# A causal convolution and a two-product mixture step on one core: the denominator's sum moved to an adding transfer, one form of the cubic, two convolution pieces, a new order

## The chip, the cores and the metric

One core of a Trainium2 chip runs the kernel. The time is that of one execution on the device in microseconds (us). The core's engines run side by side, each with its own queue in order: PE (matrix products; its weight loads are shown apart as PEld), ACT (activation functions), DVE (vector operations), POOL (GpSimd, vector operations too) and SP, which here only issues transfers. Transfers run on 16 DMA engines. PE reads from on-chip memory (SBUF) and writes to accumulators (PSUM, eight banks); ACT and DVE reach both, POOL and the transfers SBUF alone.

## The reference

x has 8 sequences of 4096 tokens with 192 columns, in 8 heads of 24. The weights of 7 taps per head are put through a softmax, and each column is convolved with its head's taps, causally. Then every token goes through a two-layer step with a rational function between:

```python
w = softmax(weight)                      # [8 heads, 7 taps]
x = conv(x, w)                           # 32768 tokens x 192
h = x @ w_in                             # 192 -> 2048
P = a[0] + a[1] * h + a[2] * h**2 + a[3] * h**3
Q = 1.0 + np.abs(b[0]) * np.abs(h) + np.abs(b[1]) * h**2
g = P / (Q + 1e-06)
out = g @ w_out                          # 2048 -> 192
```

The product weights come as float64, everything else is float32.

## The kernel before

The 32768 tokens are taken in 64 chunks of 512. For one chunk:

- **Load.** SP loads the chunk's columns (two transfers, `in_xa` and `in_xb`) in a layout with 9 blocks of 58 tokens, each with the 6 tokens ahead of it.
- **Convolution** (L259). It is a matrix product with a band of taps, for six groups of 32 columns. A matmul makes 32 columns of 58 tokens and uses one of PE's four column tiles of 32. Half 0 has four groups on the four column tiles (9 x 4 = 36 matmuls), half 1 has two groups on two column tiles (18). Steps `c0a`, `c0b`, `c0c` are the three pieces of half 0, `c1a` to `c1c` those of half 1. A float32 matmul is two records in the trace. ACT copies the result out (step `xh`, L267), rounded, and DVE subtracts the copy (`xl`, L273 and L277) to get the remainder; of half 1 both lie in one tile, the copy in partitions 0 to 63 and the remainder in 64 to 127.
- **First product** (`g1`, L289). The 2048 columns of h are made in 8 *units* of 2 x 128 columns: a unit's h is 128 partitions x 1024 numbers in two PSUM banks (tile `hp`), from 10 matmuls of 512 tokens. There are two such tiles.
- **Elementwise steps of a unit**, each over 128 x 1024 numbers. The cubic, by Horner's rule in tile `t`: `hs` copies h to SBUF (ACT, L334), `p` makes a3 h + a2 (POOL, L340, or ACT, L328), `u` multiplies by h (POOL, L347, or DVE, L345), `v` adds a1 and multiplies by h (DVE, L351). The denominator: `A` is |b0||h| (ACT, L354), `B` is |b1|h^2 (ACT, L357), `Q` adds B to A (POOL, L360). Its reciprocal: `L` takes the logarithm (ACT, L363), `Y` the exponential of minus that (ACT, L366, tile `y` in PSUM, of which there is one), and with a first product `m` (DVE, L370) the steps `e` (L375) and `g` (L379, both DVE) do one step of refinement and finish the unit's g.
- **Second product** (`g2`, L306). Per unit 128 columns x 2 are multiplied with `w_out`, in pieces `a` to `d`, for two pairs of 128 tokens one after the other; `O` (L313) copies a finished pair out, and SP stores it (L314).

`MODES` says how a unit's cubic begins: U as above on POOL; V has `p` on ACT; H has `p` on ACT and `u` on DVE, without the copy `hs`. `MODES = "UUUHVUUV"` makes five U, one H and two V units in a chunk.

The order in which the program hands steps to the engines is a table, and the scheduler keeps it: each engine runs its steps in that order, and waits for what a step needs (inputs, and a free buffer: 4 each of `t`, `A` and `B`, 3 of `hs`, 11 of `g`, 1 of the convolution's result). `PLAN` is one round of it; a step's number behind the point tells how many chunks it lags behind the chunk that the round begins. 61 rounds are run so. `START` holds the first two rounds, mixed with the preparation of the weights (steps `wi*` and `wo*`: 16 pieces are turned from float64 to float32 by integer operations on ACT, DVE and POOL), and `END` what is left at the end.

Of the kernel before, what the change touches and what calls it, by code (L numbers as in the profile page):

```python
# [62 lines left out]
wim3.0 wid4.0 wih1.0 wid3.0 g10a.0 wio2.0 wim4.0 wir2.0 g10b.0 wis4.0 wia5.0 wio4.0 hs0.0 wil1.0
wis3.0 wir4.0 g11a.0 wio3.0 wih2.0 wir3.0 wih3.0 wim5.0 p0.0 u0.0 wia6.0 g11b.0 B0.0 wil2.0 wis5.0
wil3.0 A0.0 v0.0 wim6.0 hs1.0 Q0.0 wia7.0 wio5.0 wid6.0 wid5.0 p1.0 A1.0 wim7.0 wid7.0 wir5.0 wih4.0
g12a.0 L0.0 woa2.0 wil4.0 wis6.0 wis7.0 g12b.0 wom2.0 wio7.0 c0a.1 Y0.0 c0b.1 B1.0 hs2.0 wio6.0
wih5.0 u1.0 wir6.0 B2.0 c0c.1 A2.0 m0.0 wod2.0 v1.0 p2.0 wir7.0 g13a.0 u2.0 wos2.0 e0.0 g0.0 wil5.0
g13b.0 xh0.1 woa0.0 xl0.1 wih6.0 v2.0 woa1.0 c1a.1 c1b.1 Q1.0 hs3.0 B3.0 wom0.0 g14a.0 wod0.0 A3.0
L1.0 wom1.0 Y1.0 u3.0 Q2.0 woo2.0 wor2.0 g14b.0 v3.0 p4.0 wos1.0 woo1.0 c1c.1 g15a.0 wos0.0 m1.0
woo0.0 wil6.0 e1.0 g15b.0 hs4.0 B4.0 L2.0 Q3.0 g1.0 hs5.0 A4.0 u4.0 v4.0 woa6.0 wih7.0 Y2.0 m2.0  # L70
wom6.0 g16a.0 g16b.0 wod1.0 xh1.1 wod6.0 p5.0 wor0.0 L3.0 B5.0 Q4.0 woa3.0 A5.0 e2.0 g2.0 wor1.0
woa4.0 hs6.0 u5.0 wom3.0 wos3.0 wos6.0 wil7.0 wom4.0 Y3.0 woo6.0 wod3.0 Q5.0 woo3.0 L5.0 L4.0 wos4.0
p6.0 B6.0 v5.0 m3.0 wor6.0 woa7.0 g17a.0 e3.0 g17b.0 xl1.1 g3.0 wod7.0 u6.0 A6.0 v6.0 Y4.0 m4.0
wor3.0 g10a.1 wom7.0 e4.0 g10b.1 hs7.0 wos7.0 p7.0 A7.0 woa5.0 Q6.0 hs0.1 B7.0 g4.0 Y5.0 wom5.0
# [10 lines left out]
L3.2 xl0.1 hs5.2 c1a.1 e1.2 g23c.2 g1.2 v4.2 Y2.2 g23d.2 B5.2 c1b.1 g16a.2 O0.2 p5.2 u5.2 A5.2
g16b.2 m2.2 c1c.1 g24a.2 e2.2 g2.2 g24b.2 hs6.2 Q5.2 B6.2 Y3.2 p6.2 v5.2 m3.2 g24c.2 g24d.2 g25a.2
g17a.2 g25b.2 g17b.2 A6.2 u6.2 g25c.2 e3.2 g25d.2 L5.2 L4.2 g26a.2 Q6.2 xh1.1 g3.2 xl1.1 v6.2 Y4.2
g26b.2 hs7.2 m4.2 p7.2 g10a.1 B7.2 g26c.2 e4.2 A7.2 g10b.1 g4.2 hs0.1 g26d.2 Y5.2 B0.1 u7.2 p0.1
A0.1 g27a.2 g27b.2 L6.2 u0.1 g27c.2 v7.2 g11a.1 g27d.2 O1.2 m5.2 g11b.1 Q7.2 hs1.1 p1.1 e5.2 g20a.1
g5.2 g20b.1 u1.1 Y6.2 v0.1 g20c.1 Q0.1 g12a.1 g20d.1 B1.1 L7.2 g12b.1 m6.2 A1.1 g21a.1 g21b.1 e6.2  # L90
# [6 lines left out]
g17a.1 O1.1 g21a.0 A6.1 L5.1 g17b.1 p6.1 g21b.0 g24a.0 g24b.0 Y5.1 u6.1 g24c.0 g21c.0 Q6.1 g21d.0
p7.1 m5.1 g24d.0 g25a.0 g22a.0 g25b.0 A7.1 g22b.0 g25c.0 B7.1 e5.1 g25d.0 g26a.0 L6.1 g26b.0 g5.1
Y6.1 v6.1 m6.1 hs7.1 g22c.0 g26c.0 Q7.1 g26d.0 g22d.0 L7.1 e6.1 g6.1 g23a.0 u7.1 g27a.0 g23b.0 Y7.1
v7.1 m7.1 e7.1 g7.1 g27b.0 g27c.0 g27d.0 g23c.0 O1.0 g23d.0 O0.0  # L100
# [8 lines left out]
def kernel(  # L109
# [143 lines left out]
    GROUPS = ((0, 1, 2, 3), (4, 5))  # L253

    def conv_part(c, half, cps, blks):
        for blk in blks:
            for j, g in enumerate(GROUPS[half]):
                n = min(BW, CH - blk * BW)
                nc.tensor.matmul(cps[32 * j:32 * j + 32, blk * BW:blk * BW + n], lhsT=stat(c, blk, g),  # L259
                                 rhs=wb_t[:, g, 0:n], start=True, stop=True, tile_position=(0, 32 * j))  # L260

    X = {}

    def conv_evac_act(c, half, cps):
# [2 lines left out]
        nc.scalar.copy(out=xh[0:n], in_=cps[0:n])  # L267
        X[c, "AB"[half]] = xh

    def conv_evac_dve(c, half, cps):  # L270
        if half == 0:
            xl = xpool.tile([P, CH], F32R, name="xl")
            nc.vector.tensor_tensor(out=xl, in0=cps, in1=X[c, "A"].bitcast(F32), op=ALU.subtract)  # L273
            X[c, "L"] = xl
        else:
# [1 line left out]
            nc.vector.tensor_tensor(out=xh[64:P], in0=cps[0:64], in1=xh[0:64].bitcast(F32), op=ALU.subtract)  # L277

# [80 lines left out]
    def step_Q(k):  # L359
        nc.gpsimd.tensor_tensor(out=st[k]["A"], in0=st[k]["A"], in1=st[k]["B"], op=ALU.add)  # L360
# [128 lines left out]
```

## Time and profile before

| | |
|---|---|
| median of 3 runs | 2807.57 us (2807.32 to 2807.76) |
| span of the profiled execution, which is also its time | 2807.8 us |
| PE, DVE, ACT, POOL busy | 2748.3, 2683.3, 2688.4, 2684.4 us |
| one round of 512 tokens | 42.68 us |
| DMA: bytes moved, share of the 16 engines | 64.43 MB, 8.4% |

A row of the list of groups gives line, engine, operation, output and inputs by tile name, shapes and count, then busy time in us and the mean of one in ns, then how long the engine stood idle just before them and who ended that. Busy times of neighbouring instructions overlap a little, since an engine starts the next one while the last one is still writing; for PE more so. What an instruction costs its engine is therefore read from start to start, and the rows of the timeline give starts. In the timeline a row with "x24" stands for 24 records in a row.

### The profile page before, as it was taken

The page shows a single profiled execution, that of the slowest core. Times are in us where ns is not written, and L with a number is a line of the kernel's source. Part 1 is how long each engine was busy: PE and PEld are TensorE (multiplying, and loading weights), DVE is VectorE, ACT ScalarE, POOL GpSimd, SP SyncE. Part 2 cuts the span into 40 slices and gives each one's busy share as a digit, 9 for nine tenths or more (in the row PEclk, how much of TensorE's full clock was granted, in tenths as well). Part 3 has the DMA queues.
Part 4 walks back from the last instruction along what each step waited for, and adds up shares of the span by engine and source line. Part 5 has one row for each costly group of instructions (what it writes and reads, how often), then busy time and mean ns, then how long its engine had stood idle before and what let it go on. Part 6 is the DMA issues. An engine that isn't in the chain of part 4 may idle for free.

```text
span 2807.8 us, 50193 instructions
## 1 busy us (share of the span) xinstructions
PE 2748.3 (98%) x20224; PEld 2458.2 (88%) x20224; DVE 2683.3 (96%) x2309; ACT 2688.4 (96%) x2990; POOL 2684.4 (96%) x1304
## 2 busy tenths in 40 slices
...
PEclk8899999999999999999999999999999999999999
...
DMA packets 49193, 64.43 MB, mean 23 GB/s; under 512 B 4672, under 2 KB 43840, under 8 KB 48960
## 3 DMA queue, kind: packets, MB, share of 16 engines
q1 hardware_dynamic: 48960, 61.22, 7.9%
q8 instruction: 159, 2.61, 0.4%
...
## 4 chain that ended last, share of the span: by engine, by line
PE 96%; DVE 2%; issue 1%; ACT 0%; DMA 0%; SPq 0%; ACTq 0%; DVEq 0%
PE op L306 48%; PE hp L289 42%; PE cps L259 6%; DVE ad L227 0%; PE cps L306 0%; DVE t L351 0%; DVE wl_t L245 0%; DMA g<-in_w_in 0%; DVE g L370 0%; DVE y L375 0%; DVE tr L233 0%; DVE tr L237 0%; DVE wo_t L233 0%; DVE g L379 0%; DVE wo_t L237 0%
## 5 line engine op out<-in xcount | busy, mean ns | idle before, releaser
L306 PE MATMUL op<-wo_t,g 128*128 128x192 f32 x8128 | 1420.8, 326 | 0.0
L306 PEld LDWEIGHTS op<-wo_t,g 128*128 128x128 f32 x8128 | 1344.6, 189 | 43.9
L360 POOL TENSOR_TENSOR A<-A,B 128x1024 f32<-128x1024 f32 x512 | 1219.2, 2388 | 28.4 <-ACT B L357 26.1
L347 POOL TENSOR_TENSOR t<-t,hs 128x1024 f32<-128x1024 f32 x448 | 1077.9, 2406 | 48.6 <-ACT hs L334 16.3
L289 PE MATMUL hp<-xh,wh_t 128*128 128x512 f32 x2048 | 872.9, 426 | 45.9 <-DVE t L351 41.4
L370 DVE SCALAR_TENSOR_TENSOR g<-t,cf,y 128x1024 f32<-128x1024 f32 x512 | 654.4, 1278 | 57.0 <-ACT y L366 46.6
L351 DVE SCALAR_TENSOR_TENSOR t<-t,cf,hp 128x1024 f32<-128x1024 f32 x512 | 652.5, 1274 | 32.7 <-POOL t L347 29.9
L379 DVE SCALAR_TENSOR_TENSOR g<-y,g 128x1024 f32<-128x1024 f32 x512 | 626.9, 1224 | 17.5
L289 PE MATMUL hp<-xh,wl_t 128*128 128x512 f32 x2048 | 637.7, 393 | 0.0
L375 DVE SCALAR_TENSOR_TENSOR y<-A,y 128x1024 f32<-128x1024 f32 x512 | 625.5, 1222 | 0.0
L363 ACT ACTIVATE B<-A 128x1024 f32<-128x1024 f32 x512 | 547.0, 1069 | 0.2 <-POOL A L360 0.2
L366 ACT ACTIVATE y<-B 128x1024 f32<-128x1024 f32 x512 | 528.8, 1033 | 15.6 <-DVE g L379 14.6
L354 ACT ACTIVATE A<-hp 128x1024 f32<-128x1024 f32 x512 | 528.0, 1031 | 15.8 <-PE hp L289 15.7
L357 ACT ACTIVATE B<-hp 128x1024 f32<-128x1024 f32 x512 | 528.7, 1033 | 0.0
L289 PEld LDWEIGHTS hp<-xh,wh_t 128*128 128x128 f32 x2048 | 388.8, 190 | 124.4 <-DVE t L351 32.6
L334 ACT COPY hs<-hp 128x1024 f32<-128x1024 f32 x448 | 457.2, 1020 | 35.4 <-PE hp L289 34.1
L289 PEld LDWEIGHTS hp<-xh,wl_t 128*128 128x128 f32 x2048 | 388.2, 190 | 87.5
L289 PE MATMUL hp<-xl,wh_t 128*128 128x512 f32 x1024 | 405.5, 396 | 2.4 <-DVE xl L273 2.4
L340 POOL TENSOR_SCALAR t<-hs,cf 128x1024 f32<-128x1024 f32 x320 | 389.6, 1217 | 10.8 <-ACT hs L334 3.9
L328 ACT ACTIVATE t<-hp,cf 128x1024 f32<-128x1024 f32 x192 | 214.7, 1118 | 25.3 <-PE hp L289 22.8
L259 PEld LDWEIGHTS cps<-wb_t,xs 128*32 128x32 f32 x6876 | 162.5, 149 | 65.8 <-issue 64.3
L289 PEld LDWEIGHTS hp<-xl,wh_t 128*128 128x128 f32 x1024 | 195.4, 191 | 23.7 <-DVE xl L273 2.9
...
## 6 DMA issues: line engine op xcount, KB each, us to landing
out<-ob SPq DMA_DIRECT2D x128, 192.0 KB, 2.0
...
g<-in_w_in SPq DMA_DIRECT2D x8, 512.0 KB, 9.4
...
```

The costliest lines, as they stand in the source:

```text
L289: nc.tensor.matmul(H[k][:, j, :], lhsT=w[:, i, part, j, :], rhs=x, start=(n == 0), stop=(n == len(terms) - 1))
L306: nc.tensor.matmul(op[:, t, 0:D], lhsT=g[:, f % 2, tok:tok + P], rhs=wo_t[:, f, :], start=(f == 0 and t == 0), stop=(f == FT - 1 and t == 1))
L347: nc.gpsimd.tensor_tensor(out=t, in0=t, in1=st[k]["hs"], op=ALU.mult)
L351: nc.vector.scalar_tensor_tensor(out=t, in0=t, scalar=a1, in1=flat(k), op0=ALU.add, op1=ALU.mult)
L354: nc.scalar.activation(out=tile_of(k, "A", work), in_=flat(k), func=AF.Abs, scale=r_be0)
L357: nc.scalar.activation(out=tile_of(k, "B", work), in_=flat(k), func=AF.Square, scale=r_sq1)
L360: nc.gpsimd.tensor_tensor(out=st[k]["A"], in0=st[k]["A"], in1=st[k]["B"], op=ALU.add)
L363: nc.scalar.activation(out=st[k]["B"], in_=st[k]["A"], func=AF.Ln, bias=C_Q)
L366: nc.scalar.activation(out=tile_of(k, "y", ps_y), in_=st[k]["B"], func=AF.Exp, scale=-1.0)
L370: nc.vector.scalar_tensor_tensor(out=G[k].rearrange("p a b -> p (a b)"), in0=st[k]["t"], scalar=a0, in1=st[k]["y"], op0=ALU.add, op1=ALU.mult)
L375: nc.vector.scalar_tensor_tensor(out=y, in0=st[k]["A"], scalar=C_Q, in1=y, op0=ALU.add, op1=ALU.mult)
L379: nc.vector.scalar_tensor_tensor(out=g, in0=st[k]["y"], scalar=2.0, in1=g, op0=ALU.subtract, op1=ALU.mult)
```

## The change

Four things are changed together.

1. `Q`: the addition of B to A on POOL is replaced by a transfer that POOL issues, from SBUF to SBUF, with addition at its destination. The data are 128 x 1024 float32, 512 KB, per unit.
2. `MODES` is all U: `hs` on ACT, `p` and `u` on POOL in all eight units.
3. Each half of the convolution is one piece. Half 1 uses four column tiles: its two groups for blocks 0 to 4 on the first two (partitions 0 to 63 of the result, tokens 0 to 289), for blocks 5 to 8 on the other two (partitions 64 to 127, tokens 290 to 511). Its copy and its subtraction are two instructions each, of 64 partitions x 290 and x 222; the remainder goes into the other 64 partitions of the same tokens.
4. `PLAN`, `START` and `END` are written anew.

```diff
-MODES = "UUUHVUUV"
+MODES = "UUUUUUUU"
...
-c0a.0 L7.2 m6.2 u1.1 g12a.1 O1.2 A1.1 e6.2 g12b.1 B1.1 Q0.1 g6.2 g20a.1 hs2.1 c0b.0 v1.1 g20b.1 Y7.2
+c0.0 O1.2 Q1.1 hs2.1 v1.1 Y7.2 p2.1 g20a.1 B2.1 m7.2 g20b.1 u2.1 g13a.1 A2.1 e7.2 L0.1 g13b.1 g7.2 xh0.0
...
-    def conv_part(c, half, cps, blks):
-        for blk in blks:
-            for j, g in enumerate(GROUPS[half]):
-                n = min(BW, CH - blk * BW)
-                nc.tensor.matmul(cps[32 * j:32 * j + 32, blk * BW:blk * BW + n], lhsT=stat(c, blk, g),
-                                 rhs=wb_t[:, g, 0:n], start=True, stop=True, tile_position=(0, 32 * j))
+    CUT = -(-NBLK // 2)
+    TOK = CUT * BW
+
+    def conv_part(c, half, cps):
+        if half == 0:
+            tiles = [(blk, g, g) for blk in range(NBLK) for g in range(4)]
+        else:
+            tiles = [(b + s * CUT, g, 2 * s + g - 4) for b in range(CUT) for s in range(2) for g in (4, 5)
+                     if b + s * CUT < NBLK]
+        for blk, g, j in tiles:
+            n = min(BW, CH - blk * BW)
+            nc.tensor.matmul(cps[32 * j:32 * j + 32, blk * BW:blk * BW + n], lhsT=stat(c, blk, g),
+                             rhs=wb_t[:, g, 0:n], start=True, stop=True, tile_position=(0, 32 * j))
...
+    LOW, UP = (slice(0, 64), slice(0, TOK)), (slice(64, P), slice(TOK, CH))
...
-        n = 32 * len(GROUPS[half])
-        nc.scalar.copy(out=xh[0:n], in_=cps[0:n])
+        if half == 0:
+            nc.scalar.copy(out=xh, in_=cps)
+        else:
+            for p in (LOW, UP):
+                nc.scalar.copy(out=xh[p], in_=cps[p])
...
-            nc.vector.tensor_tensor(out=xh[64:P], in0=cps[0:64], in1=xh[0:64].bitcast(F32), op=ALU.subtract)
+            for p, q in ((LOW, (slice(64, P), LOW[1])), (UP, (slice(0, 64), UP[1]))):
+                nc.vector.tensor_tensor(out=xh[q], in0=cps[p], in1=xh[p].bitcast(F32), op=ALU.subtract)
...
     def step_Q(k):
-        nc.gpsimd.tensor_tensor(out=st[k]["A"], in0=st[k]["A"], in1=st[k]["B"], op=ALU.add)
+        nc.gpsimd.dma_start(out=st[k]["A"], in_=st[k]["B"], accum_op=ALU.add)
...
-    def conv_step(c, half, piece):
-        if piece == 0:
-            if half == 0 and 0 < c < NCH - 1:
-                load_x(c + 1)
...
+    def conv_step(c, half):
+        if half == 0 and 0 < c < NCH - 1:
+            load_x(c + 1)
```

How the order moves shows at three places. On PE, the later two pieces of half 0 before (`cps` is the convolution's result, `op` the second product's, `hp` h; a row here is a matmul, half the records of the trace):

```order
L289 MATMUL hp<-xh_11965,wl_t 128x512
L306 MATMUL op<-wo_t,g 128x192 x2
L259 MATMUL cps<-wb_t,xs_98 32x58 x12
L306 MATMUL op<-wo_t,g 128x192 x2
L259 MATMUL cps<-wb_t,xs_98 32x58 x8
L259 MATMUL cps<-wb_t,xs_98 32x48 x4
L289 MATMUL hp<-xh_11848,wh_t 128x512
```

And PE at half 0 after the change:

```order
L298 MATMUL hp<-xh_12088,wl_t 128x512
L263 MATMUL cps<-wb_t,xs_98 32x58 x32
L263 MATMUL cps<-wb_t,xs_98 32x48 x4
L315 MATMUL op<-wo_t,g 128x192 x4
L298 MATMUL hp<-xh_11919,wh_t 128x512
```

The 36 matmuls of half 0 now stand in one row, between a first and a second product.

On POOL, two units before, the second of them one whose linear step is not on POOL:

```order
L340 TENSOR_SCALAR t<-hs,cf 128x1024
L347 TENSOR_TENSOR t<-t,hs 128x1024
L360 TENSOR_TENSOR A<-A,B 128x1024
L347 TENSOR_TENSOR t<-t,hs 128x1024
L360 TENSOR_TENSOR A<-A,B 128x1024
```

And POOL after it, where `DMA` is the issue of the adding transfer:

```order
L356 TENSOR_TENSOR t<-t,hs 128x1024
L349 TENSOR_SCALAR t<-hs,cf 128x1024
L369 DMA A<-B 128x1024
L356 TENSOR_TENSOR t<-t,hs 128x1024
L369 DMA A<-B 128x1024
L349 TENSOR_SCALAR t<-hs,cf 128x1024
```

Each unit now has a linear step, a product and an issue on POOL, in a changing order.

On ACT, from the step B of a chunk's last unit to that unit's logarithm, before (B, A, then L5, hs, Y5, A, B, L6, hs, Y6, and the unit's own L):

```order
L357 ACTIVATE B<-hp 128x1024
L354 ACTIVATE A<-hp 128x1024
L363 ACTIVATE B<-A 128x1024
L334 COPY hs<-hp 128x1024
L366 ACTIVATE y<-B 128x1024
L354 ACTIVATE A<-hp 128x1024
L357 ACTIVATE B<-hp 128x1024
L363 ACTIVATE B<-A 128x1024
L334 COPY hs<-hp 128x1024
L366 ACTIVATE y<-B 128x1024
L363 ACTIVATE B<-A 128x1024
```

And the same stretch after, where B is the later of the two inputs:

```order
L366 ACTIVATE B<-hp 128x1024
L343 COPY hs<-hp 128x1024
L375 ACTIVATE y<-B 128x1024
L366 ACTIVATE B<-hp 128x1024
L363 ACTIVATE A<-hp 128x1024
L372 ACTIVATE B<-A 128x1024
L343 COPY hs<-hp 128x1024
L375 ACTIVATE y<-B 128x1024
L372 ACTIVATE B<-A 128x1024
```

The logarithm of the unit before has moved ahead of the unit's A and B, so seven instructions stand between its inputs and its logarithm, where eight stood.

More of the change, by code (lines that the diff above doesn't have):

```diff
@@ new lines @@
+g20c.1 hs3.1 v2.1 g20d.1 Y0.1 g21a.1 p3.1 g21b.1 A3.1 m0.1 g14a.1 Q2.1 B3.1 e0.1 u3.1 g14b.1 L1.1 g0.1
+g21c.1 hs4.1 g21d.1 Q3.1 Y1.1 v3.1 g22a.1 g22b.1 B4.1 p4.1 m1.1 g22c.1 A4.1 g15a.1 u4.1 e1.1 L2.1 g15b.1
+g1.1 g22d.1 hs5.1 Q4.1 v4.1 g23a.1 Y2.1 g23b.1 p5.1 xl0.0 g23c.1 B5.1 m2.1 g23d.1 u5.1 L3.1 g16a.1 e2.1
+O0.1 A5.1 g16b.1 g2.1 Q5.1 g24a.1 hs6.1 v5.1 g24b.1 Y3.1 g24c.1 p6.1 c1.0 A6.1 m3.1 u6.1 g17a.1 L4.1
+e3.1 xh1.0 g17b.1 B6.1 g3.1 g24d.1 hs7.1 g25a.1 xl1.0 g25b.1 Y4.1 p7.1 v6.1 g25c.1 A7.1 g25d.1 m4.1 Q6.1
@@ L63 @@
[L63 to L74, printed above, removed]
@@ new lines @@
+B1.0 p1.0 g12b.0 wil3.0 wih4.0 c0.1 u1.0 A2.0 wim6.0 wil4.0 hs2.0 wis6.0 A1.0 p2.0 wio6.0 wid7.0 wim7.0
+L0.0 wir5.0 v1.0 Y0.0 Q1.0 wis7.0 g13a.0 woa0.0 u2.0 B2.0 m0.0 g13b.0 wom0.0 e0.0 hs3.0 Q2.0 wid6.0
+wio7.0 p3.0 B3.0 g0.0 L1.0 wir7.0 wos0.0 Y1.0 wir6.0 woo0.0 A3.0 v2.0 u3.0 wih5.0 m1.0 woa1.0 g14a.0
+woa2.0 xh0.1 wil5.0 g14b.0 wod0.0 Q3.0 wom1.0 hs4.0 wor0.0 e1.0 A4.0 p4.0 v3.0 wih7.0 woa3.0 xl0.1
+g15a.0 wod1.0 g1.0 B4.0 g15b.0 wom2.0 Q4.0 L3.0 wom3.0 wos1.0 u4.0 wih6.0 hs5.0 wos2.0 wil7.0 A5.0 p5.0
@@ new lines @@
+L2.0 wos3.0 woo1.0 B5.0 u5.0 wil6.0 Y2.0 v4.0 wor1.0 m2.0 g16a.0 woa4.0 woo3.0 g16b.0 e2.0 hs6.0 g2.0
+p6.0 woo2.0 Y3.0 v5.0 u6.0 B6.0 wom4.0 g17a.0 wod3.0 wos4.0 A6.0 m3.0 Q5.0 g17b.0 wod2.0 wod4.0 Q6.0
+c1.1 e3.0 L4.0 wor3.0 hs7.0 g3.0 wor2.0 xh1.1 woo4.0 A7.0 v6.0 wor4.0 woa5.0 Y4.0 p7.0 xl1.1 B7.0 wom5.0
+g10a.1 u7.0 m4.0 woa6.0 L5.0 g10b.1 e4.0 L6.0 Q7.0 g4.0 wod5.0 v7.0 Y5.0 wod6.0 wom6.0 g11a.1 woa7.0
+wos5.0 hs0.1 m5.0 g11b.1 A0.1 p0.1 e5.0 B0.1 u0.1 L7.0 wom7.0 woo5.0 hs1.1 wos6.0 B1.1 wos7.0 p1.1 g5.0
@@ L85 @@
[L85 to L90, printed above, removed]
@@ L97 @@
[L97 to L100, printed above, removed]
+c0.1 O1.3 Q1.2 hs2.2 v1.2 Y7.3 p2.2 g20a.2 B2.2 m7.3 g20b.2 u2.2 g13a.2 A2.2 e7.3 L0.2 g13b.2 g7.3
+g20c.2 hs3.2 v2.2 g20d.2 Y0.2 g21a.2 p3.2 g21b.2 B3.2 m0.2 g21c.2 u3.2 A3.2 g21d.2 e0.2 g14a.2 L1.2 g0.2
@@ new lines @@
+Y5.2 p0.1 g27c.2 m5.2 g27d.2 u0.1 g11a.1 O1.2 e5.2 B0.1 g11b.1 L6.2 g5.2 Q0.1 g20a.1 hs1.1 v0.1 g20b.1
+Y6.2 g20c.1 p1.1 g20d.1 L7.2 m6.2 g12a.1 u1.1 A1.1 e6.2 g12b.1 B1.1 g6.2 g21a.1 hs2.1 g21b.1 v1.1 Y7.2
+g21c.1 p2.1 g21d.1 B2.1 m7.2 g22a.1 Q1.1 A2.1 g13a.1 e7.2 u2.1 L0.1 g13b.1 g7.2 g22b.1 hs3.1 Q2.1 v2.1
+g22c.1 Y0.1 g22d.1 p3.1 g23a.1 A3.1 m0.1 g14a.1 u3.1 B3.1 e0.1 g14b.1 L1.1 g0.1 g23b.1 hs4.1 Q3.1 g23c.1
+v3.1 Y1.1 g23d.1 p4.1 g20a.0 O0.1 m1.1 L2.1 g20b.0 u4.1 g24a.1 e1.1 A4.1 g24b.1 B4.1 g15a.1 g1.1 Q4.1
```

50 lines of the change are left out of this document (23 added, 27 removed).

## The prediction

> **What bounds the kernel now.** I read the page first: the span, the busy shares and the chain that ended last.
>
> ```profile
> span 2807.8 us, 50193 instructions
> ...
> PE 2748.3 (98%) x20224; PEld 2458.2 (88%) x20224; DVE 2683.3 (96%) x2309; ACT 2688.4 (96%) x2990; POOL 2684.4 (96%) x1304
> ...
> PEclk8899999999999999999999999999999999999999
> ...
> PE 96%; DVE 2%; issue 1%; ACT 0%; DMA 0%; SPq 0%; ACTq 0%; DVEq 0%
> ```
>
> Four engines are at 96% or more, but the chain is PE for 96% of the span, so PE sets the end. The clock row is at full speed behind the first two slices. Next come the waits between 200 and 2600 us, and the busy time of one round of 512 tokens, from one copy of an output to the same copy a round later.
>
> ```profile
> PEld cps L259 <- issue: 50.4, 224, 0.2
> DVE g L370 <- ACT y L366: 35.8, 113, 0.5
> DVE t L351 <- POOL t L347: 26.4, 110, 0.4
> POOL A L360 <- ACT B L357: 24.1, 57, 0.5
> ```
>
> ```profile
> 1404.03:1446.71 42.68, 42.68 (x318) 38.26 (x317) 41.07 (x36) 41.61 (x48) 41.52 (x21) 1.00 0.08 21
> ```
>
> A round takes 42.68 us. The columns behind it are PE, PEld, DVE, ACT and POOL: PE is busy in all of it, the other three leave only 1.1 to 1.6 us. PE itself waits for no engine; its one gap, in front of the convolution (L259), is its own, 224 times, four a round. So the round is the sum of PE's starts, and the others fit with little to spare. In the start it is otherwise:
>
> ```profile
> 0.00:124.00 124.00, 68.15 (x495) 53.71 (x496) 113.83 (x119) 89.36 (x118) 95.09 (x58) 0.81 0.25 77
> ```
>
> There DVE, with the weights to prepare, is busy for 113.83 of 124 us and PE for 68: what PE saves there is not seen.
>
> **The convolution, the term that pays.** These are PE's rows around a piece of the second half (x36) and three of the first (x24), and a long stretch of the second product.
>
> ```profile
> 1405.94 2.11 PE L306 MATMUL op<-wo_t,g 128*128 128x192 f32 x12
> 1407.98 1.29 PE L259 MATMUL cps<-wb_t,xs 128*32 128x58 f32 x36
> 1409.20 0.50 PE L289 MATMUL hp<-xh,wh_t 128*128 128x512 f32 x1
> ...
> 1424.74 0.59 PE L259 MATMUL cps<-wb_t,xs 128*32 128x58 f32 x24
> 1425.26 0.50 PE L289 MATMUL hp<-xh,wh_t 128*128 128x512 f32 x1
> ...
> 1427.67 0.81 PE L306 MATMUL op<-wo_t,g 128*128 128x192 f32 x4
> 1428.41 0.59 PE L259 MATMUL cps<-wb_t,xs 128*32 128x58 f32 x24
> 1428.93 0.92 PE L306 MATMUL op<-wo_t,g 128*128 128x192 f32 x4
> 1429.78 0.58 PE L259 MATMUL cps<-wb_t,xs 128*32 128x58 f32 x24
> ...
> 1437.55 4.06 PE L306 MATMUL op<-wo_t,g 128*128 128x192 f32 x24
> 1441.32 0.53 PE L289 MATMUL hp<-xh,wh_t 128*128 128x512 f32 x1
> ```
>
> From start to next start, the x36 piece takes 1.22 us and an x24 piece 0.52. A matmul here is two records. The x36 runs on two column tiles, so it is 18 steps; the x24 runs on four, so it is 6. The difference gives (1.22 - 0.52) / 12 = 0.058 us a step, whether two or four tiles work in it, and 0.52 - 6 x 0.058 = 0.17 us fixed. Around a piece more is lost: four records of the second product take 4 x (1441.32 - 1437.55) / 24 = 0.63 us in a long stretch, but 0.74 ahead of a piece and 0.85 between two, so about 0.11 on either side. A piece costs 0.17 + 0.22 = 0.39 us beside its steps. The change makes two pieces of four, which is 0.78 us, and ten steps of the second half's 18 (nine blocks become five positions, two records each), which is 0.46. Together 1.24 us; I take 1.2, because a piece between two kinds of product may lose a little less than one inside the second product. PE's round becomes 41.5 us.
>
> **What the other engines then hold.** The page's groups that are added or removed, and two more from the list of groups by shape:
>
> ```profile
> L360 POOL TENSOR_TENSOR A<-A,B 128x1024 f32<-128x1024 f32 x512 | 1219.2, 2388 | 28.4 <-ACT B L357 26.1
> L347 POOL TENSOR_TENSOR t<-t,hs 128x1024 f32<-128x1024 f32 x448 | 1077.9, 2406 | 48.6 <-ACT hs L334 16.3
> ...
> L340 POOL TENSOR_SCALAR t<-hs,cf 128x1024 f32<-128x1024 f32 x320 | 389.6, 1217 | 10.8 <-ACT hs L334 3.9
> L328 ACT ACTIVATE t<-hp,cf 128x1024 f32<-128x1024 f32 x192 | 214.7, 1118 | 25.3 <-PE hp L289 22.8
> ```
>
> ```profile
> L345 DVE TENSOR_TENSOR t<-t,hp 128x1024 f32<-128x1024 f32 x64 | 77.4, 1210 | 0.0
> L277 DVE TENSOR_TENSOR xh<-cps,xh 64x512 fp32r<-64x512 f32 x63 | 43.1, 683 | 2.0
> ```
>
> ACT loses two linear steps a round (the V units, 2 x 1.12) and its copy of the second half becomes two smaller ones; I give that 0.3 us, between nothing and a whole copy again. The H unit's linear step becomes a copy of about the same length. 41.61 - 2.24 + 0.3 = 39.7. DVE loses the H unit's product (1.21) and gains a second subtraction, between nothing and 0.68, say 0.25, since both together cover the same 512 columns: 41.07 - 1.21 + 0.25 = 40.1. Both stay under 41.5, with about the slack that they have now.
>
> POOL loses eight adds (8 x 2.39 = 19.1) and gains one product (2.41) and three linear steps (3 x 1.22): 41.52 - 19.1 + 2.4 + 3.7 = 28.5 us, plus the issue of eight transfers. No row shows POOL issuing one. The nearest rows are SP's:
>
> ```profile
> 1404.54 0.38 SPq L314 DMA_DIRECT2D out<-ob  x1
> 1409.31 0.47 SPq L158 DMA_DIRECT2D xs<-in_xa  x1
> 1409.84 0.59 SPq L159 DMA_DIRECT2D xs<-in_xb  x1
> ```
>
> The low end is 0.38 us. The high end is the add's own 2.39, which would give POOL 47.6 us a round and the kernel 61 x (47.6 - 42.68) = 300 us more. I take 1.2, twice SP's dearest row, because a transfer that adds names two rows to read and one to write: POOL 38.1 us. The value hardly matters until (41.5 - 28.5) / 8 = 1.62 us, and the time is the old one at (42.68 - 28.5) / 8 = 1.77.
>
> **The transfer.** It replaces a step that ended 2.39 us after its start. Its issue waits on POOL for both of ACT's results, as the add did, with the next unit's linear step and product queued behind it; for its landing wait ACT's logarithm (L363, and behind it all of ACT) and later DVE's correction (L375). SP's loads and stores keep their places beside the convolution and the output copy. How fast transfers are, two stretches of the start show (the last two columns: share of the 16 engines, GB/s), then the page's issues (us to landing):
>
> ```profile
> 10.00:20.00 10.00, 3.11 (x40) 2.12 (x32) 8.77 (x14) 8.05 (x14) 2.71 (x3) 1.00 1.03 348
> 20.00:30.00 10.00, 4.77 (x17) 3.44 (x15) 9.83 (x10) 5.74 (x8) 7.55 (x5) 0.94 1.08 322
> ```
>
> ```profile
> out<-ob SPq DMA_DIRECT2D x128, 192.0 KB, 2.0
> ...
> g<-in_w_in SPq DMA_DIRECT2D x8, 512.0 KB, 9.4
> ```
>
> With the DMA engines full (share over 1) they moved 322 to 348 GB/s. 192 KB landed in 2.0 us, of which 0.6 is moving, so 1.4 is fixed. 0.52 MB is then 1.6 us of all engines if a row read and added counts once, and 3.1 if both rows read count. The low end of the landing is 3.0 us, the high end the 9.4 of the queued weights; I take the doubled reading, because the add needs both rows in the transfer: 1.4 + 3.1 = 4.5, and 5.7 with the issue. Against it stands what ACT does meanwhile:
>
> ```profile
> 1404.39 1.05 ACT L357 ACTIVATE B<-hp 128x1024 f32<-128x1024 f32 x1
> ...
> 1409.05 1.06 ACT L354 ACTIVATE A<-hp 128x1024 f32<-128x1024 f32 x1
> ```
>
> Five starts between these two make (1409.05 - 1404.39) / 5 = 0.93 us an instruction. ACT's new order has seven to eleven of them between the later of A and B and its unit's logarithm: 6.5 us at the tightest, mostly over 8. With one product ahead of the issue on POOL (2.4) the transfer needs up to 8.1. So in a full round ACT hardly waits, and has 1.8 us of slack for it. A landing of 9.4 would be 4 us beyond the tightest place; the distance spans some three units, so there would be two or three such waits a round, about 10 us: 51.5 a round, 3345 us. Per round the engines are taken for 8 x 3.1 plus today's 0.08 x 42.68 = 3.4: 28 of 41.5 us.
>
> The Trainium skill (DMA: Bandwidth & Descriptors, section on the anatomy of a GpSimd DMA) gives 2.0 us plus the bytes at 436 GB/s, which is an estimate of 3.2 us for 512 KB; and Collectives: The Full Stack (section on the bandwidth ceiling) says that a reduce is half as fast as a copy because it reads two sources, not because of the add. Together 4.4 us, the same sum as by my 4.5, where the row of 9.4 gives 3345; no run here shows an adding transfer yet.
>
> **The sum.** 61 full rounds x 1.2 = 73 us off. The first and last units' chains grow by 5.7 - 2.4 = 3.3 us each, partly covered: 5 us on. From the span, 2807.8 (0.2 over the runs' median of 2807.57): 2807.6 - 73 + 5 = 2739.6 us.
>
> **Rivals.** *The issue on POOL is dear (the other side).* At 2.0 us POOL needs 44.5 a round and everything waits on it: 2807.6 + 61 x 1.8 = 2918. For it speaks that POOL can be held by DVE in the start:
>
> ```profile
> 12.86 1.29 POOL L241 TENSOR_TENSOR tr<-tr,ad 128x512 int32<-128x512 int32 x1 [8.73 <-ACT xh L267]
> ...
> 12.60 0.42 DVE L227 TENSOR_SCALAR ad<-ad 128x512 f32<-128x512 f32 x1
> 13.05 1.38 DVE L233 TENSOR_SCALAR tr<-ad 128x512 uint32<-128x512 uint32 x1
> ```
>
> The DVE step that met POOL's add took 1.38 instead of 0.42 and ended 0.28 us behind the add. If DVE's big steps (1.2 us, nearly without a break) held the issue so, each would wait half of one more, 1.2 + 0.6 = 1.8. Against it: in full rounds POOL's steps keep their 2.4 and 1.2 us while DVE is 96% busy. It decides from 1.77. The Trainium skill (SBUF — State Buffer, "Who interferes with whom") says that two-port forms such as tensor_scalar lock GpSimd out for a whole instruction; the start agrees, and the full rounds' DVE instructions are of other forms.
>
> *The DMA engines become the bound.* If an added row costs three passes (1.57 MB) at the page's mean, 61.22 MB in 7.9% of the span, 276 GB/s, a transfer takes 5.7 us; 8 x 5.7 + 3.4 = 49 a round, 3190 us. It decides from (42.68 - 3.4) / 8 = 4.9 us. Against it: 322 GB/s above.
>
> ```profile
> q1 hardware_dynamic: 48960, 61.22, 7.9%
> ```
>
> *The gain is eaten in part.* DVE's 40.1 of 41.5, or late landings, cost half a microsecond to one a round: 2765 to 2800. Here too belongs that the change doesn't do what it says: if the second half's four tiles went two abreast, only 0.78 a round is left, 2765.
>
> **Chances.** The forecast, 2725 to 2765: 0.68 (the low end has 64 rounds and a start relieved by 5 us). Eaten in part: 0.10. No change: 0.04. Dear issue: 0.09. DMA-bound: 0.09. A difference under 0.2% (5.6 us) can't be told from none. Faster 0.78, same 0.04, slower 0.18. The range 2725 to 2830 takes in the first three and the mild third of the fourth, about 0.83.
>
> **What would show it.** Right: a round of 41.3 to 41.7 us with PE busy throughout, L259's gap 128 times instead of 256, POOL down to about two thirds busy without its issues, DMA share near 0.65. Wrong in a size: POOL's issues over 1.62 us back to back; ACT's logarithm waiting for the landing; a DMA share near 1.

## The result, and the profile after

The changed kernel takes 2743.18 us (median of 4 runs, 2740.07 to 2745.52), the kernel before 2807.66 on the same chip. The ratio is 0.9769, with a 95% interval of 0.9755 to 0.9783: 64.5 us or 2.3% faster, 3 us from the 2740 foretold.

The page of the changed kernel: the span, the busy shares, the clock and DMA rows in 40 slices, the two DMA queues and the chain that ended last.

```profile
span 2740.2 us, 51286 instructions
...
PE 2683.1 (98%) x20224; PEld 2420.2 (88%) x20224; DVE 2618.3 (96%) x2309; ACT 2563.2 (94%) x2926; POOL 2305.8 (84%) x1560
...
PEclk7899999999999999999999999999999999999999
DMA  6466566666656666666665666666566666666654
...
q0 software_dynamic: 73728, 268.47, 52.0%
q1 hardware_dynamic: 48960, 61.22, 8.0%
...
PE 95%; DVE 2%; issue 1%; POOL 1%; ACT 1%; DMA 0%; SPq 0%; POOLq 0%; DVEq 0%; ACTq 0%
```

PE still is the chain, with 95% of a shorter span, and its busy time fell by 65.2 us. POOL is no longer at 96%. A new queue, q0, carries the 512 adding transfers and takes half of the DMA engines' time; the DMA row shows five to six tenths in the full rounds, and the clock row stands at full speed from the third slice on, as before.

One round of the changed kernel, from an output copy to the same copy a round later (PE, PEld, DVE, ACT, POOL, granted clock, DMA share, GB/s):

```profile
1413.00:1454.58 41.58, 41.58 (x318) 37.63 (x317) 40.02 (x36) 39.63 (x46) 35.58 (x25) 1.00 0.61 122
```

The round went from 42.68 to 41.58 us. Over the whole run its median is 41.59 against 42.67, so 61 rounds give 61 x 1.08 = 66 of the 67.6 us by which the profiled span is shorter. Nearly nothing lies outside of them: the first output copy comes 0.9 us earlier (122.8 instead of 123.7), the stretch behind the last one is as long as it was (3.7 and 3.6 us).

PE's rows around the two pieces of the convolution in the changed kernel, which answer to the x36 and x24 rows of before:

```profile
1416.63 0.84 PE L263 MATMUL cps<-wb_t,xs 128*32 128x58 f32 x36
1417.40 0.50 PE L298 MATMUL hp<-xh,wh_t 128*128 128x512 f32 x1
...
1435.20 1.34 PE L263 MATMUL cps<-wb_t,xs 128*32 128x58 f32 x72
1436.46 1.57 PE L315 MATMUL op<-wo_t,g 128*128 128x192 f32 x8
```

Half 1 on four tiles takes 0.77 us instead of 1.22, half 0 in one piece 1.26 instead of 3 x 0.52 = 1.56. That is 0.75 us from the pieces themselves. The rest of the round's 1.08 lies beside them. Adding up PE's rows from start to next start over 20 rounds, from 800 us on, gives the second product 20.05 us a round instead of 20.59, since it is cut less often (0.54 less), but the first product 19.51 instead of 19.30 (0.21 more): -0.75 - 0.54 + 0.21 = -1.08. Why the first product is slower in the new order isn't shown.

The waits of the changed kernel between 200 and 2600 us (total, times, longest):

```profile
POOL t L349 <- ACT hs L343: 256.6, 339, 1.7
ACT hs L343 <- PE hp L298: 98.2, 173, 0.8
DVE g L379 <- ACT y L375: 55.4, 119, 1.0
POOL A L369 <- ACT A L363: 45.4, 99, 0.6
PEld cps L263 <- issue: 32.7, 113, 0.4
```

Before the convolution PE's own gap comes 113 times instead of 224, but each is now 32.7 / 113 = 0.29 us instead of 0.23. POOL's room shows as a wait for ACT's copy `hs`, 256.6 / 57.7 rounds = 4.4 us a round. No engine waits long for the transfer: the page's groups of the changed kernel, with its issue and the logarithm that needs it, and the issues' time to landing:

```profile
L372 ACT ACTIVATE B<-A 128x1024 f32<-128x1024 f32 x512 | 550.9, 1076 | 4.2 <-DMA A<-B 4.2
...
L369 POOL DMA_DIRECT2D A<-B x512 | 479.8, 938 | 69.4 <-ACT A L363 53.2
...
A<-B POOLq DMA_DIRECT2D x512, 512.0 KB, 4.8
```

512 logarithms waited 4.2 us in all. An issue takes 0.94 us in the mean (median 0.88, 0.85 to 1.18) and the sum has landed 4.8 us after the issue began.

### The profile page after: what moved, and what is told of

It reads as the page before. It is cut to its first block, busy times and chain, and to the rows that moved or that the text cites. A ratio compares the mean times of both kernels' runs of the same rounds, so it can differ in the third digit from the quotient of the medians.

```text
span 2740.2 us, 51286 instructions
## 1 busy us (share of the span) xinstructions
PE 2683.1 (98%) x20224; PEld 2420.2 (88%) x20224; DVE 2618.3 (96%) x2309; ACT 2563.2 (94%) x2926; POOL 2305.8 (84%) x1560
## 4 chain that ended last, share of the span: by engine, by line
PE 95%; DVE 2%; issue 1%; POOL 1%; ACT 1%; DMA 0%; SPq 0%; POOLq 0%; DVEq 0%; ACTq 0%
PE op L315 48%; PE hp L298 42%; PE cps L263 5%; DVE t L360 0%; PE cps L315 0%; POOL t L356 0%; DVE ad L224 0%; DVE y L384 0%; DVE wl_t L242 0%; DVE g L379 0%; DVE tr L230 0%; POOL t L349 0%; DMA xs<-in_xb 0%; DVE tr L234 0%; ACT ad L220 0%
## 5 line engine op out<-in xcount | busy, mean ns | idle before, releaser
L315 PEld LDWEIGHTS op<-wo_t,g 128*128 128x128 f32 x8128 | 1342.0, 190 | 39.7
L356 POOL TENSOR_TENSOR t<-t,hs 128x1024 f32<-128x1024 f32 x512 | 1267.3, 2475 | 31.8
L349 POOL TENSOR_SCALAR t<-hs,cf 128x1024 f32<-128x1024 f32 x512 | 648.4, 1266 | 302.5 <-ACT hs L343 296.6
L343 ACT COPY hs<-hp 128x1024 f32<-128x1024 f32 x512 | 524.4, 1024 | 133.5 <-PE hp L298 122.1
L375 ACT ACTIVATE y<-B 128x1024 f32<-128x1024 f32 x512 | 536.1, 1047 | 9.7 <-DVE g L388 5.4
L369 POOL DMA_DIRECT2D A<-B x512 | 479.8, 938 | 69.4 <-ACT A L363 53.2
L263 PEld LDWEIGHTS cps<-wb_t,xs 128*32 128x32 f32 x6876 | 122.8, 151 | 37.1 <-issue 36.6
L263 PE MATMUL cps<-wb_t,xs 128*32 128x58 f32 x6876 | 139.2, 229 | 0.0
```

The source lines that it names most:

```text
L315: nc.tensor.matmul(op[:, t, 0:D], lhsT=g[:, f % 2, tok:tok + P], rhs=wo_t[:, f, :], start=(f == 0 and t == 0), stop=(f == FT - 1 and t == 1))
L349: nc.gpsimd.tensor_scalar(tile_of(k, "t", work), st[k]["hs"], a3, a2, ALU.mult, ALU.add)
L356: nc.gpsimd.tensor_tensor(out=t, in0=t, in1=st[k]["hs"], op=ALU.mult)
L375: nc.scalar.activation(out=tile_of(k, "y", ps_y), in_=st[k]["B"], func=AF.Exp, scale=-1.0)
```

## The experiments

The question was which of the four parts carry the 64 us: the shorter convolution alone, with the other parts as bystanders (theory 1), or the parts only together. Each kernel was measured against the kernel before; its ratio stands with its 95% interval.

### The convolution alone

The kernel before, with the new convolution and nothing else; the order keeps its rows, a merged piece standing where its first stood.

```diff
-c0a.0 L7.2 m6.2 u1.1 g12a.1 O1.2 A1.1 e6.2 g12b.1 B1.1 Q0.1 g6.2 g20a.1 hs2.1 c0b.0 v1.1 g20b.1 Y7.2
-c0c.0 p2.1 L0.1 m7.2 g13a.1 B2.1
+c0.0 L7.2 m6.2 u1.1 g12a.1 O1.2 A1.1 e6.2 g12b.1 B1.1 Q0.1 g6.2 g20a.1 hs2.1 v1.1 g20b.1 Y7.2
+p2.1 L0.1 m7.2 g13a.1 B2.1
...
-... v5.1 c1a.0 c1b.0 L4.1 c1c.0 p6.1
+... v5.1 c1.0 L4.1 p6.1
```

> The kernel before with the convolution of the change alone (two pieces, four column tiles); its order, its adds on POOL and its three forms of the cubic stay, with each half's piece where the first of its three stood. Theory 1 (PE's sum of starts sets the round, and each part of the change pays by itself): 1.1 us a round less, 2807.6 - 61 x 1.1 = 2741 us. Rival (before, POOL's starts add up to 8 x 2.36 + 7 x 2.36 + 5 x 1.28 = 41.8 us a round, so POOL takes over as soon as PE is shorter): at the best 41.8 to 42.0 a round, 2755 to 2765. Second rival (the old order was fitted to the old pieces, and the longer piece meets its neighbours at the wrong moment): no gain, 2800 or more.

2842.02 us, ratio 1.012 (1.0105 to 1.0136): 34 us *slower* than before. Its page and its waits between 200 and 2600 us:

```profile
PE 2723.4 (96%) x20224; PEld 2413.9 (85%) x20224; DVE 2689.8 (95%) x2373; ACT 2692.4 (95%) x3054; POOL 2681.9 (94%) x1304
...
POOL 34%; PE 21%; DVE 20%; issue 16%; ACT 8%; DMA 0%; POOLq 0%; SPq 0%; DVEq 0%; ACTq 0%
```

```profile
DVE g L380 <- ACT y L376: 75.5, 56, 1.4
ACT hs L344 <- PE hp L299: 61.4, 55, 1.2
PEld hp L299 <- DVE t L361: 57.4, 55, 1.1
...
POOL A L370 <- ACT B L367: 38.6, 56, 0.7
```

PE's busy time did fall, by 25 us, and still the run is longer. The chain goes round POOL, PE, DVE and ACT: once a round (55 and 56 times) PE waits for DVE's `v` to free a tile of h, ACT for that tile, POOL for ACT's `B`, DVE for ACT's `y`. No engine is full: the round is 43.24 us in the median, while ACT, the fullest beside PE, is busy for 41.7 of it, and POOL's starts add up to 41.8. Half 1's second copy and second subtraction lengthen ACT's and DVE's busy time by only 0.1 us a round, so their size doesn't explain the loss either. What is left is the order: the steps as they stood, with PE's work moved, seem to form a circle that is longer than any engine's sum. That is read from the chain and the waits; no run moved a single step of the old order. Theory 1 falls here.

### Half 1 on two tiles again

```diff
-            tiles = [(b + s * CUT, g, 2 * s + g - 4) for b in range(CUT) for s in range(2) for g in (4, 5)
-                     if b + s * CUT < NBLK]
+            tiles = [(b, g, g - 4) for b in range(NBLK) for g in (4, 5)]
```

(The copies and subtractions keep their sizes and read partitions 0 to 63.)

> The changed kernel with the second half of the convolution on two column tiles again, still one piece: 18 steps for 10. Theory 1 (0.058 us a step, PE sets the round): 8 x 0.058 x 61 = 28 us more than the changed kernel, 2771. Rival (other engines have become the bound at 41.6 us, or PE's steps on two tiles are covered): under 10 us more.

2771.65 us, ratio 0.9871 (0.9856 to 0.9887); the round is 42.07 us, 0.48 more. The eight steps (18 against 10) cost 0.06 us each, as the rows of before gave (0.058).

### Half 0 in three pieces again

```diff
-c0.0 O1.2 Q1.1 hs2.1 v1.1 Y7.2 p2.1 g20a.1 B2.1 m7.2 g20b.1 u2.1
+c0a.0 O1.2 Q1.1 hs2.1 v1.1 Y7.2 p2.1 g20a.1 c0b.0 B2.1 m7.2 g20b.1 c0c.0 u2.1
```

> The changed kernel with half 0 of the convolution in three pieces again, the second and third behind the next two pieces of the second product. Theory 1 (a piece costs 0.25 to 0.39 us of PE beside its steps): two more pieces, 61 x 0.5 to 0.78 = 30 to 48 us more, 2773 to 2791. Rival (what was gained came from POOL and the order, and a piece costs only the 0.2 us of its gap): 61 x 0.4 = 24 us or less.

2787.45 us, ratio 0.9924 (0.9909 to 0.9939); the round is 42.31 us, 0.72 more, 0.36 for each piece. The gap ahead of the convolution in this kernel is back to 225 times:

```profile
PEld cps L263 <- issue: 57.8, 225, 0.4
```

With the experiment before, the two parts of the convolution are worth 28 + 44 = 72 us in the new order, against 64.5 for the whole change: on PE the gain is all the convolution, and the first product's 0.21 us a round goes the other way.

### Half 0 between two pieces of the second product

To see whether a piece costs more between two kinds of product, `c0` was moved behind `g20b`, and the output copy `O1` ahead so that it doesn't have to wait.

```diff
-c0.0 O1.2 Q1.1 hs2.1 v1.1 Y7.2 p2.1 g20a.1 B2.1 m7.2 g20b.1 u2.1
+Q1.1 hs2.1 v1.1 Y7.2 p2.1 g20a.1 B2.1 m7.2 g20b.1 c0.0 u2.1
...
-... L7.1 m6.1
+... L7.1 O1.1 m6.1
```

> The changed kernel with the first half's piece moved behind the next two pieces of the second product, so that it stands in front of a first product as the second half's does, and with the copy of the finished output (O1) moved up behind that chunk's last logarithm. In the changed kernel's rows the piece in front of a second product costs 0.42 us beside its steps (1.265 - 18 x 0.058 = 0.22, 0.09 ahead, 0.11 behind), that in front of a first product 0.25. If the neighbour sets that cost: 61 x 0.17 = 10 us less, 2733. If a piece costs the same anywhere: 2743 as the changed kernel, or a little more where the second product now waits for the copy of its bank.

2744.63 us, ratio 0.9771 (0.9758 to 0.9785): no change. The gap ahead of the convolution in this kernel became smaller,

```profile
PEld cps L263 <- issue: 25.6, 114, 0.2
```

and nothing was won. By PE's rows over 20 rounds the first product takes 0.08 us a round less here than in the changed kernel and the second 0.12 more, so the cost moved from one neighbour to the other. The likely reason, which is only argued: the switch between the two products, at which the piece stood, is now a place of its own. A gap named in the list of waits isn't by itself a cost that can be saved.

### The three forms kept

The changed kernel with the old forms of the cubic (five U, one H, two V); the order stays the new one.

```diff
-MODES = "UUUUUUUU"
+MODES = "UUUHVUUV"
```

> The changed kernel with the three forms of the cubic as before (one H and two V units a chunk), in the new order; a linear step stands on ACT where POOL's stood, and the H unit's on ACT in place of its copy. Theory A (sums: an engine binds when its own work exceeds PE's 41.6 us a round): ACT 39.6 + 2.1 = 41.7, DVE 40.0 + 1.2 = 41.2, POOL falls to 29: 41.8 to 42 a round, 2755 to 2770 us. Theory B (the order decides: what the convolution alone showed, a step put where the order left no room for it makes PE wait): 43 or more a round, 2830 or more.

2833.16 us, ratio 1.0091 (1.0074 to 1.0108). A round of this kernel, its chain and the first of its waits:

```profile
1394.69:1437.65 42.96, 42.38 (x321) 37.53 (x324) 41.06 (x37) 41.42 (x48) 29.80 (x21) 1.00 0.60 119
```

```profile
ACT 37%; issue 32%; DVE 18%; POOL 10%; PE 3%; POOLq 0%; DMA 0%; SPq 0%; ACTq 0%; DVEq 0%
```

```profile
POOL t L358 <- ACT t L337: 368.8, 112, 5.5
POOL A L371 <- ACT B L368: 206.3, 68, 3.7
```

POOL is busy for 29.8 of 42.96 us and all the same is one of the engines on the chain: twice a round it stands before a product whose linear step ACT has not come to (368.8 us in 112 waits, up to 5.5), with the issues of other units' transfers queued behind it. ACT, which took over the linear steps, has the largest share of the chain, and is still busy for only 41.42 us of the round: the order in which the steps wait for each other is longer than any sum, as theory B had it. Which of the moved steps costs how much isn't separated.

### The old order with the rest

The changed kernel with the order tables of before (pieces merged; the linear steps that are new on POOL right behind their `hs`). One row of either order:

```diff
-g20c.1 hs3.1 v2.1 g20d.1 Y0.1 g21a.1 p3.1 g21b.1 A3.1 m0.1 g14a.1 Q2.1 B3.1 e0.1 u3.1 g14b.1 L1.1 g0.1
+g21b.1 B3.1 m0.1 g14a.1 hs3.1 p3.1 Q3.1 g14b.1 e0.1 L1.1 g21c.1 g0.1 g21d.1 Q2.1 g22a.1 u3.1 Y1.1
```

> The order of before with all the rest of the change: adding transfer, all units in form U, two convolution pieces on four tiles; each linear step stands right behind its unit's copy. Theory A (sums): nothing lost, 2743 us. Theory B (the order decides; in the old order the logarithm follows its add as closely as POOL's 2.4 us allowed, and the landing now takes 4.8): ACT waits for landings and PE for ACT and DVE, 45 us a round or more, 2950 or more.

3130.09 us, ratio 1.115 (1.1132 to 1.1169). A round of this kernel, its chain and its waits:

```profile
1412.83:1460.82 47.99, 43.86 (x317) 38.64 (x316) 40.09 (x36) 40.03 (x47) 35.47 (x25) 0.96 0.53 106
```

```profile
PE 59%; POOL 17%; issue 14%; DVE 5%; ACT 3%; DMA 1%; SPq 0%; POOLq 0%; ACTq 0%; DVEq 0%
```

```profile
POOL t L350 <- ACT hs L344: 537.6, 300, 4.5
PEld hp L299 <- DVE t L361: 225.3, 105, 3.6
...
ACT B L373 <- DMA A<-B: 169.5, 103, 2.8
```

DVE, ACT and POOL hold as much as in the changed kernel (40.0, 39.6 and 35.6), but the round is 6.4 us longer. Here ACT does wait for the landing, twice a round and up to 2.8 us: at these places the old order left the sum too few steps of cover. But the larger waits are POOL's for ACT's copy and PE's for DVE's `v`, and the chain has the transfers at 1% and POOL at 17%. So the old order doesn't carry the new forms and the transfer; how much of the 6.4 us is due to the landing and how much to the linear steps that POOL now has in this order isn't separated.

### The addition back on POOL

```diff
-        nc.gpsimd.dma_start(out=st[k]["A"], in_=st[k]["B"], accum_op=ALU.add)
+        nc.gpsimd.tensor_tensor(out=st[k]["A"], in0=st[k]["A"], in1=st[k]["B"], op=ALU.add)
```

> The changed kernel with the addition of A and B back on POOL, in the new order. POOL's starts: 8 x (2.36 + 1.28 + 2.36) = 48.0 us a round. If POOL's sum decides: 2743 + 61 x 6.4 = 3133 us, POOL at 99%. If the new order has other weaknesses with a slow sum: more than 3180.

3125.30 us, ratio 1.1127 (1.111 to 1.1144). A round of this kernel:

```profile
1397.81:1445.57 47.76, 43.53 (x318) 37.39 (x317) 40.12 (x36) 40.41 (x46) 47.26 (x25) 1.00 0.07 19
```

POOL is busy for 47.26 of 47.76 us. The issue in place of the addition is what lets POOL take all eight units. It isn't shown that the gain needs this: no run has the new convolution with the old three forms and POOL's addition in an order fitted to them. By POOL's starts, 41.8 us a round, such a kernel could come to 2755 to 2765 us, as the first experiment's expectation said.

### Two issues a unit

The same bytes in two transfers of 512 columns.

```diff
-        nc.gpsimd.dma_start(out=st[k]["A"], in_=st[k]["B"], accum_op=ALU.add)
+        for half in (slice(0, CH), slice(CH, W)):
+            nc.gpsimd.dma_start(out=st[k]["A"][:, half], in_=st[k]["B"][:, half], accum_op=ALU.add)
```

> The changed kernel with each adding transfer issued as two of 512 columns. If an issue costs POOL the same whatever its bytes (0.88 us by the changed kernel's rows), POOL's round goes from 28.5 + 8 x 0.88 = 35.6 to 42.6 us: POOL takes over as the bound a little above the old round's time, 2743 + 61 x 1.0 = 2805 us or up to 20 more. If the issue's cost goes with the bytes: 2743 and POOL's share unchanged. A third way, if the prediction's point of 1.62 us is too high: over 2830.

2866.40 us, ratio 1.021 (1.0193 to 1.0227), a round of 43.53 us in the median. First POOL's rows in the changed kernel, from start to start a product of 2.36 us, an issue with a wait, and a linear step of 1.27; then this kernel's chain, its group of issues and two of its rows:

```profile
1401.28 0.86 POOL L369 DMA_DIRECT2D A<-B  x1
1401.92 2.65 POOL L356 TENSOR_TENSOR t<-t,hs 128x1024 f32<-128x1024 f32 x1
...
1406.73 2.41 POOL L356 TENSOR_TENSOR t<-t,hs 128x1024 f32<-128x1024 f32 x1
1409.09 0.87 POOL L369 DMA_DIRECT2D A<-B  x1
1410.40 1.19 POOL L349 TENSOR_SCALAR t<-hs,cf 128x1024 f32<-128x1024 f32 x1 [0.44 <-ACT hs L343]
1411.67 2.40 POOL L356 TENSOR_TENSOR t<-t,hs 128x1024 f32<-128x1024 f32 x1
```

```profile
POOL 49%; issue 21%; DVE 18%; ACT 7%; PE 4%; DMA 1%; POOLq 0%; SPq 0%; DVEq 0%; ACTq 0%
...
L370 POOL DMA_DIRECT2D A<-B x1024 | 978.1, 1160 | 10.4 <-ACT B L366 5.4
```

```profile
1401.38 1.76 POOL L370 DMA_DIRECT2D A<-B  x2
1402.56 3.01 POOL L356 TENSOR_TENSOR t<-t,hs 128x1024 f32<-128x1024 f32 x1
```

An issue of half the bytes isn't shorter: the shortest takes 0.83 us here and 0.85 in the changed kernel, and with one issue to a unit the mean is 938 ns for either size (next experiment). POOL's sum is 8 x (2.36 + 1.27) = 29.0, and 16 issues at 0.88 make it 43.1, near the 43.5 measured, and POOL leads the chain: it has become the bound. With two issues to a unit the price per unit is 1.76 us, and the time is already above the old one; the prediction put that point at 1.77. From 29.0 instead of its 28.5 (busy means of instructions that overlap, less what overlaps) the issue matters from (41.6 - 29.0) / 8 = 1.57 and gives the old time at (42.68 - 29.0) / 8 = 1.71.

### Half of the bytes

One issue as before, for 512 of the 1024 columns; the other half of the denominator's sum is left out.

```diff
-        nc.gpsimd.dma_start(out=st[k]["A"], in_=st[k]["B"], accum_op=ALU.add)
+        nc.gpsimd.dma_start(out=st[k]["A"][:, 0:CH], in_=st[k]["B"][:, 0:CH], accum_op=ALU.add)
```

> The changed kernel with the adding transfer over 512 of the 1024 columns only; the other half of the denominator's sum is left out. Half the bytes, the same number of issues. If the transfer is hidden wholly: 2743, with a shorter landing (about 1.4 + 1.4 to 2 us + issue) and half the DMA share. If landings hold ACT or the traffic slows other engines: 5 us less or more.

2742.85 us, ratio 0.9765 (0.9748 to 0.9781), the time of the changed kernel. Of this kernel, the queue and the time to landing:

```profile
q0 software_dynamic: 73728, 134.25, 28.6%
...
A<-B POOLq DMA_DIRECT2D x512, 256.0 KB, 3.3
```

The sum lands 1.5 us earlier and nobody has use for it: the transfer of the changed kernel is hidden. Half the bytes cost the DMA engines more than half: 28.6% x 2741.6 us / 512 = 1.53 us of all 16 engines.

### A copy beside each transfer, and two

SP copies each unit's finished g, 512 KB, to a scratch tile, of which there are two in turn; then twice.

```diff
+        for _ in range(1):
+            nc.sync.dma_start(out=scr.tile([P, W], F32, name="sc"), in_=g)
```

> The changed kernel with one more transfer per unit: SP copies the unit's finished g (512 KB) from SBUF to a spare tile, so each adding transfer shares the 16 engines with about one plain copy. The adding transfers hold 52% of the engines now, 2.8 us each; a copy at the start's 340 GB/s is 1.5 us: 8 x 4.3 + 3.4 = 38 of 41.6 us, under the engines' bound. If the landing has the room that the prediction gave it (6.5 us at the tightest, from A and B to the logarithm, against 4.8 now): 10 us more or less, 2743 to 2755. If the room is smaller (the old order lost 390 us with the same 4.6 us landing): ACT waits for landings of 6 us, 43 a round or more, 2830 or more.

> As the run with one copy per unit, with two. The engines' sum becomes 8 x (2.8 + 3.0) + 3.4 = 50 us a round: if the DMA engines then bind as the second rival of the prediction had it, 2743 + 61 x 8.4 = 3255 us, with the DMA share near 1 and ACT waiting for landings. If transfers overlap better than their packets' times add up: under 3000.

One copy: 2743.62 us, ratio 0.9766 (0.9752 to 0.9781), no change, although the sum now lands after 5.6 us. The stretch from 200 to 2600 us of this kernel, and its two queues:

```profile
200.00:2600.00 2400.00, 2399.26 (x18196) 2169.32 (x18195) 2308.16 (x2020) 2285.49 (x2595) 2053.78 (x1386) 1.00 0.88 223
```

```profile
q0 software_dynamic: 73728, 268.47, 51.8%
q1 hardware_dynamic: 122688, 329.68, 34.0%
```

The DMA engines have room up to a share of 0.88. A plain copy takes (34.0 - 8.0)% of 2743.3 us / 512 = 1.39 us of all engines, an adding transfer of the same bytes 52.0% x 2740.2 / 512 = 2.78: twice as much, which is the doubled reading of the prediction. The copies were issued by SP on another queue; no run has a plain copy issued by POOL, so that the whole factor comes from the addition isn't shown.

Two copies: 3089.81 us, ratio 1.1004 (1.0987 to 1.102). The same stretch of this kernel, its chain and its landing:

```profile
200.00:2600.00 2400.00, 2223.79 (x16176) 1971.15 (x16175) 2062.96 (x1795) 2046.47 (x2308) 1832.97 (x1231) 0.97 1.00 285
```

```profile
DMA 96%; DVE 2%; issue 1%; ACT 0%; PE 0%; SPq 0%; POOL 0%; ACTq 0%; POOLq 0%; DVEq 0%
...
A<-B POOLq DMA_DIRECT2D x512, 512.0 KB, 7.4
```

At a share of 1.00 the transfers are the chain, and the sum lands after 7.4 us. The engines' sum, 8 x (2.78 + 2 x 1.39) + 8% x 42 = 47.8 us a round, fits the 46.9 measured; the expected 3255 us was too high, in part because it put a copy at 1.5 us. This looks like the prediction's DMA rival, brought about by a load that the change doesn't have, but another limit lies at the same place: 95% of the chain are the copies alone, one behind the other, and SP waits 2042 us in all for an earlier copy to leave one of the two scratch tiles, with the loads and stores queued behind. Full engines and these two tiles aren't told apart by this run.

### A step of the start on POOL

The preparation's maximum for the `w_out` pieces was moved from DVE, the fullest engine of the start, to POOL.

```diff
-            nc.vector.tensor_scalar(w["a"].bitcast(F32), w["a"].bitcast(F32), F64_MIN, None, ALU.max)
+            eng = nc.vector if which == "i" else nc.gpsimd
+            eng.tensor_scalar(w["a"].bitcast(F32), w["a"].bitcast(F32), F64_MIN, None, ALU.max)
```

> The changed kernel with one step of the weights' preparation (the maximum, for the eight pieces of the second product's weights) on POOL for DVE. The start's first 100 us have DVE busy for 98% and POOL for 80%, and this step takes DVE 8 x 0.81 = 6.5 us. If DVE sets the start's length: 4 to 7 us less, about 2738. If POOL's order is held up by the step, or POOL's use of the shared port slows DVE's other steps by as much: 2743 or more.

2747.76 us, ratio 0.9784 (0.9771 to 0.9797), 5 us behind the changed kernel and not ahead of it; the round is the same, the first output copy comes at 127.5 instead of 122.8. Not all of that need be due to the edit: with half of the bytes, where the start's order is unchanged, that copy came at 124.1. The next step of these pieces in the changed kernel, then this kernel's two:

```profile
L230 DVE TENSOR_SCALAR wo_t<-ad 128x384 uint32<-128x384 uint32 x8 | 4.0, 521 | 0.0
```

```profile
L225 POOL TENSOR_SCALAR ad<-ad 128x384 f32<-128x384 f32 x8 | 10.7, 1344 | 0.0
L231 DVE TENSOR_SCALAR wo_t<-ad 128x384 uint32<-128x384 uint32 x8 | 8.8, 1101 | 9.0 <-POOL ad L225 9.0
```

DVE got rid of eight steps, and instead waits 9.0 us for POOL's and takes twice as long for the next. The order had these two steps one behind the other for one engine. No kernel of these is measurably faster than the changed one.

## Why the prediction was right, point by point

- **PE bounds the kernel, the round is its sum.** Right: 41.58 us with PE busy in all of it, against 41.5 and the 41.3 to 41.7 named.
- **The convolution is worth 1.24 us a round, taken as 1.2.** The terms are shown one by one: eight steps 0.48 (0.46 was said), two pieces 0.72 (0.78 was said). Together 1.20, but the round fell by 1.08. The rows over 20 rounds show where the rest went: the convolution and the second product became 1.29 us shorter, and the first product 0.21 us longer, 13 us in all. For that the sum has no term; it took the first product as unchanged.
- **Five microseconds more for the first and last chains.** Not seen: in the profiled executions the start and the end are as long as before, within 1 us. It is luck that this error and the missing 0.1 us a round (7 us) cancel, so that 2740 is closer than its terms.
- **ACT 39.7, DVE 40.1, POOL 38.1.** 39.6, 40.0 and 35.6; POOL's is lower mainly because the issue costs 0.94, not 1.2. The value hardly matters, as was said, but the point from which it does was put too high: 1.57 and 1.71 by POOL's starts, not 1.62 and 1.77.
- **The others fit, since their sums are under PE's.** The result bore it out, but the reason isn't enough. In the convolution alone, with the forms kept and in the old order, all sums are under the round too, and 25 to 322 us are lost against the kernel before. That the new order closes its circles in time couldn't be read from sums; this is the step that was weakest, and the rival "eaten in part" had it only as a small size.
- **Transfer 4.5 us, 5.7 with the issue, hidden by ACT's 6.5 and more.** 4.8 with the issue, and 4.2 us of waiting in the whole run. Its DMA time was put at 3.1 and is 2.78, the share at 0.65 and is 0.61. The Trainium skill's two rules that the prediction put together (DMA: Bandwidth & Descriptors, on the anatomy of a GpSimd DMA, and Collectives: The Full Stack, on the bandwidth ceiling) give an estimate of 4.4 us. The trace has 4.8, and the factor of two between an adding transfer and a copy is there in the queues' shares, with the copy issued on another queue.
- **Rivals.** Dear issue: the mechanism exists and was brought about with two issues, not with one; DVE, 96% busy, doesn't hold an issue (0.85 to 1.18 us). The rows of the start that the prediction showed as a sign of such holding have DVE's step lengthened (1.38 us) and not POOL's add, which began first and took its usual 1.3 us. DMA-bound: not up to a share of 0.88. Half 1 two abreast: it goes four abreast, 0.77 us instead of 1.22. The chances of the rivals within the range 2725 to 2830 add up to 0.85 with the forecast's, not to 0.83.
